# Low halves of the output weights and next-block sums formed on GpSimd instead of VectorE in the first output-layer stretch

## The chip, the cores and the metric

The kernel runs on one core of a Trainium2 chip. The metric is the device time of one execution in microseconds (us). The engines are named as the profile names them: PE is TensorE (PEld its weight loads), DVE is VectorE, ACT is ScalarE, POOL is GpSimd, SP is SyncE, which here only issues DMAs.

## The reference

The kernel computes attention through 32 packed queries per head, and two token-wise layers on the result:

```python
p_packed = sm_attn(p, k, v)
out = sm_attn(q, p_packed, p_packed)             # batch 8, heads 8, seq 576, head_dim 64
x = out.transpose(0, 2, 1, 3).reshape(4608, 512)
h = np.maximum(np.maximum(x @ w1, x @ w2), x @ w3)
x2 = h @ w_out                                   # 768 -> 512
h = x2 @ w_in                                    # 512 -> 2048
g = np.maximum(h, 0.0) + np.log1p(np.exp(-np.abs(h)))
return g @ w_out2                                # 2048 -> 512
```

Only the last two products, `x2 @ w_in` with its softplus and `g @ w_out2`, bear on the change.

## The kernel before, in words

The first 500 us or so do attention and the max-out layer, batch by batch, and store x2 in DRAM (`x2d`). After that the tokens are taken in five blocks: three of 2 x 512 columns and two of 2 x 384. In each block `layer3` (PE line 1044) forms the hidden layer, and `layer4` (PE line 1137) the output. Both use a seven-product scheme for 2x2 block matrices (`PRODUCTS`), so operands are sums of blocks: `form` (line 1101) makes the sums S1 to S4 of the hidden tiles, `sum_x2` (line 884) those of the next block's operand.

Every operand of a product is given in two parts, a high part rounded to PE's 32-bit format and a low part, the remainder. Three matmuls stand for one: high by high, high by low, low by high. The two parts are made by `split`: ACT copies the source into the high tile (line 126), and an engine, DVE unless another is named, subtracts it from the source (line 128). That second instruction is a TENSOR_TENSOR with two SBUF inputs.

`layer4` has 28 steps, v = 0 to 27, four for each product, each of 12 matmuls of 128x128 by 128x512. The operand of step v + 3 is split behind step v (`split_g`: `ghi` by ACT, `glo` by DVE); three buffers hold it, so its ACT copy waits until PE is done with step v. Eight weight tiles `wc` of the output layer (numbers 8 to 15) are used in order, one for 3.5 steps.

In the first block only, the output weights don't yet exist in split form. They are loaded from `wof` (`load_weights`, SP line 998) into `wu`, split into `wc` in a first part of 1024 columns and a second of 768 (`split_weights`), and stored for the later blocks (`put_weights`, SP line 1019). Tiles 8 and 9 are split in the layer before; the stretch splits 10 to 15, at steps 1, 4, 8, 11, 15 and 18. In the same stretch the operand of the second block is made in four parts of 128 columns: `load_x2` (SP line 923), `sum_x2` (four instructions of 128x256), `split_x2` (two ACT copies, two DVE subtractions into `x2lo`). `wu` and the operand tile `xu` share a pool of two buffers, so each next load waits until the split of the tile before in that buffer is done.

The order on every engine, the DMA queue of SP included, is the order in which this code is written (`tc.manual_schedule`). It comes from `jobs` (what is emitted behind each step) and `done` (sums and results of finished products). Behind each step come, in this order, `split_g(v + 3)`, the entries of `done`, and those of `jobs`:

```python
for v in range(NV):
    layer4(c, v)
    if v + 3 < NV:
        split_g(c, v + 3)
    for fn, *args in done.get(v, []) + jobs[v]:
        fn(*args)
```

Of the kernel before, what the change touches and what calls it, by code (L numbers as in the profile page):

```python
# [19 lines left out]
def packed_attention_maxout_softplus(  # L20
# [22 lines left out]
    nc = tc.nc  # L43
# [31 lines left out]
    FP = F2 // 2  # L75
# [45 lines left out]
    def split(src, hi, lo, engine=nc.vector):  # L121
        for _ in split_steps(src, hi, lo, engine):
            pass

    def split_steps(src, hi, lo, engine=nc.vector):
        nc.scalar.activation(out=hi, in_=src, func=AF.Copy)  # L126
        yield
        engine.tensor_tensor(out=lo, in0=src, in1=hi.bitcast(F32), op=ALU.subtract)  # L128
# [712 lines left out]
    for n in range(1, B):  # L841
        for slot in range(F1 + KC):
# [22 lines left out]
            if n + 1 == B:  # L865

                if slot == 0:
# [37 lines left out]
                    def pair_tile(s):  # L905
                        t = ring[s % 3].tile([P, 2, 7, 2, P], F32R, tag="ring", name="wc")
                        pairs[s] = t
                        return t
# [97 lines left out]
        elif s < STEP:  # L1006
            load_units(s - FP)

    def split_weights(s, part):
        if part == 0:  # L1010
            pair_tile(s)
        a, b = ((0, 4), (4, 7))[part]
        u, t = wus[s], pairs[s]
        split(u[:, a + 1 : b + 1], t[:, 0, a:b], t[:, 1, a:b])
        if part == 1:
            wus.pop(s)

# [6 lines left out]
    def get_weights(s):  # L1024
        if STEP <= s < STEP * NCH:
            r = s % STEP
            nc.sync.dma_start(
                out=pair_tile(s).rearrange("p h a k x -> p (h a k x)").bitcast(F32),
                in_=(wic[r] if r < FP else woc[r - FP]),
            )  # L1030
# [16 lines left out]
    def layer3(c, j, aside):  # L1047


        def between(at):  # L1050
            for fn, *args in aside.get(at, ()):
                fn(*args)

        w, wide = pairs.pop(STEP * c + j), BLOCKS[c][1]
        h = cp.tile([P, 10, CH], F32, tag="h", name="h")[:, :, :wide]

        def plus(o, a, ps):
            add(out=h[:, o], in0=h[:, a], in1=ps, op=ALU.add)  # L1058

        nc.scalar.activation(out=h[:, 3], in_=product(c, w, 0, 0), func=AF.Copy)  # L1060
        between(0)
        plus(0, 3, product(c, w, 1, 1))
        plus(4, 3, product(c, w, 4, 4))
        between(1)
        ps = product(c, w, 3, 3)
        plus(5, 4, ps)
        plus(6, 4, product(c, w, 5, 5))
        plus(3, 6, ps)
        between(2)
        plus(2, 6, product(c, w, 2, 6))  # L1070
        plus(1, 5, product(c, w, 6, 2))
        between(3)
        for half in range(2):
            for k in range(2):
                if j == 0:
                    g[half, k] = ap.tile(
                        [P, FP, CH], F32, tag=f"a{half}{k}", name=f"a{half}{k}"
                    )
                nc.scalar.activation(  # L1079
                    out=g[half, k][:, j, :wide], in_=h[:, 2 * k + half], func=AF.Softplus  # L1080
                )
# [5 lines left out]
    def form(c, name, u, n, engine):  # L1087


        us = slice(u, u + n)  # L1090
        a11, a12, a21, a22 = (
            g[i, k][:, us, : BLOCKS[c][1]] for i in range(2) for k in range(2)
        )
        s2 = None if name == "S3" else row(c, 1 + u // 2)
        out, in0, in1, op = {
            "S3": (a21, a11, a21, ALU.subtract),
            "S2": (s2, a22, a21, ALU.subtract),
            "S1": (a11, a11, s2, ALU.add),
            "S4": (a12, a12, s2, ALU.subtract),
        }[name]  # L1100
        engine.tensor_tensor(out=out, in0=in0, in1=in1, op=op)  # L1101
# [93 lines left out]
    with tc.manual_schedule(engines={E.PE, E.DVE, E.Activation, E.Pool, E.SP}):  # L1195
        for c in range(NCH):
            more, last = parts[c + 1], c == NCH - 1
            for j in range(FP):
                aside = {0: [], 1: [], 2: [], 3: []}
                if c == 0:  # L1200
                    if j + 2 < FP:
                        aside[0].append((sum_pair, j + 2, nc.gpsimd))
                    for part in range(2):
                        aside[1 + part].append((split_weights, j + 2, part))
                    aside[3] += [(load_weights, j + 4), (put_weights, j + 2)]
                    if j and j % 2 == 0:
                        aside[1].append((form, c, "S3", j - 2, 2, nc.vector))
                elif more:
                    for part in range(2):
                        if j == 1 + part:  # L1210
                            aside[0].append((load_x2, c + 1, part))
                        if j == 3 + part:
                            aside[1].append((sum_x2, c + 1, part, nc.gpsimd))
                if j == FP - 1:
                    for v in range(2):
                        aside[2].append((split_g, c, v))
                layer3(c, j, aside)
                if c:
                    form(c, "S3", j, 1, nc.gpsimd)
                get_weights(STEP * c + j + 3)  # L1220
            mid[c] = cp.tile([P, 10 * CH], F32, tag="h", name="mid")
            split_g(c, 2)
            jobs = {v: [] for v in range(-1, NV)}
            if c == 0:
                jobs[0].append((form, c, "S3", FP - 2, 2, nc.vector))
                for t in range(6):
                    v = 7 * t // 2 + 1
                    for part in range(2):
                        jobs[v + part].append((split_weights, FP + t + 2, part))
                    if t >= 1 and FP + t + 3 < STEP:  # L1230
                        jobs[v + 1].append((load_weights, FP + t + 3))
                    if t == 0:
                        jobs[v + 1].append((load_x2, c + 1, 0))
                    jobs[v + 2].append((put_weights, FP + t + 2))
                for part, v in enumerate((7, 12, 16, 21)):
                    jobs[v - 1].append((sum_x2, c + 1, part))
                    jobs[v].append((split_x2, c + 1, part))
                    if part + 1 < more:
                        jobs[v].append((load_x2, c + 1, part + 1))
            else:  # L1240
                for part, v in zip(range(more), (12, 14, 18, 22)):
                    if part > 1:
                        jobs[v - 1].append((sum_x2, c + 1, part))
                    jobs[v].append((split_x2, c + 1, part))
                    if part + 2 < more:
                        jobs[v].append((load_x2, c + 1, part + 2))
            for i in range(NU):
                for name, v in (("S2", 0), ("S1", 4), ("S4", 8)):
                    jobs[v + i].append((form, c, name, 2 * i, 2, nc.vector))
            done = {  # L1250
                3: [(keep_sum, c, "X", 0)],
                11: [(keep_sum, c, "X", 1)],
                13: [(out_tile, c, 0), (result, c, 0, 0, "Z", 0)],
                15: [(keep_sum, c, "Y", 2)],
                19: [(out_tile, c, 1), (result, c, 1, 1, "X", 2)],
                23: [(result, c, 0, 1, "Y", 1)],
                24: [(store, c, 0, (0, 1), [nc.sync, nc.scalar] if last else [nc.sync])],
                27: [(result, c, 1, 0, "X")],
            }
            if last:  # L1260
                done[19].append((store, c, 1, (1,), [nc.sync]))
                done[27].append((store, c, 1, (0,), [nc.sync, nc.scalar]))
            else:
                done[27].append((store, c, 1, (0, 1), [nc.sync]))
# [6 lines that stand above are left out]
                for t in range(FP):  # L1271
                    if (7 * t + 6) // 2 == v:
                        pairs.pop(STEP * c + FP + t)
                        get_weights(STEP * c + FP + t + 3)
# [36 lines left out]
```

## Time and profile before

| | us |
|---|---|
| median of 3 timed runs (lowest, highest) | 1230.43 (1228.89, 1233.96) |
| span of the profiled execution, first to last instruction | 1227.1 |
| first output-layer stretch (583.4 to 676.0) | 92.6 |
| second output-layer stretch, same 336 matmuls (752.2 to 831.0) | 78.8 |

The profile is of one execution, of which the page gives the span; its lines are read as follows. Busy time of an engine is the time in which an instruction of it ran; a row of a timeline gives start, duration and instruction, and in brackets how long the engine sat idle before it and what ended that. The duration of one instruction reaches a little over the start of the next one on the same engine; from start to start is the pitch. The span is 3.3 us below the median of the timed runs.

### The profile page before, as it was taken

The numbers are of one execution on the slowest core, as the hardware profiler recorded it, in microseconds if no ns is written. First come the engines' busy times: TensorE is split into PE (matmuls) and PEld (weight loads), VectorE is DVE, ScalarE is ACT, GpSimd is POOL, SyncE is SP. The second block draws the span as 40 slices with busy tenths as digits, with TensorE's granted clock in tenths as the row PEclk, the third lists the DMA queues.
The fourth block names the chain that finished last, engine by engine and source line by source line (L and its number), as shares of the span: only waits on it lengthen the run. The fifth ranks groups of instructions, "written<-read, shape, count | busy, mean of one in ns | idle before, by whom it ended". The sixth has DMA issues, their size and how long they took to land.

```text
span 1227.1 us, 21279 instructions
## 1 busy us (share of the span) xinstructions
PE 1202.3 (98%) x8599; PEld 1057.2 (86%) x8599; DVE 833.6 (68%) x1182; ACT 527.8 (43%) x782; POOL 217.9 (18%) x224
## 2 busy tenths in 40 slices
PE   8899999999999999999979999999999999999998
PEld 6788989898989899988757888888888899999998
DVE  2975757575757658677998447884468745884585
ACT  4744443434343434545554234542344423542343
POOL 1422312123333322240000030000310012000100
PEclk9999999999999999999999999999999999999999
DMA  9988585869695931767667955459554597668764
GB/s 236 278 216 207 152 208 174 204 200 232 194 262 171 235 104 35 266 259 261 220 244 271 327 199 205 159 201 329 188 196 171 191 357 279 241 230 320 251 254 146
DMA packets 117282, 272.25 MB, mean 222 GB/s; under 512 B 14784, under 2 KB 90304, under 8 KB 106944
## 3 DMA queue, kind: packets, MB, share of 16 engines
q1 hardware_dynamic: 110944, 260.87, 66.7%
q10 hardware_dynamic: 6240, 10.03, 2.3%
q8 instruction: 67, 1.10, 0.4%
q14 instruction: 31, 0.25, 0.1%
HBM read 211.09 MB, written 59.77 MB: 221 GB/s over the span
## 4 chain that ended last, share of the span: by engine, by line
PE 84%; DVE 8%; DMA 5%; issue 1%; ACT 1%; SPq 1%; DVEq 0%; ACTq 0%
PE ps L482 29%; PE ps L1044 27%; PE ps L1137 22%; DMA qraw<-in_q_dram 3%; DVE glo L128 2%; PE ps_w L460 2%; PE ps_s L287 1%; DVE wc L128 1%; DMA wu<-wof 1%; DMA wc<-wic 1%; DVE x2lo L128 1%; PE ps_e L331 1%; PE ps_v L358 1%; DVE a L1101 1%; PE ps_k L232 0%
## 5 line engine op out<-in xcount | busy, mean ns | idle before, releaser
L1137 PE MATMUL ps<-ghi,wc 128*128 128x512 f32 (+1 forms) x1120 | 328.3, 374 | 0.5 <-ACT ghi L126 0.5
L1044 PE MATMUL ps<-x2hi,wc 128*128 128x512 f32 (+1 forms) x1120 | 322.2, 367 | 0.9 <-DMA wc<-wic 0.9
L1058 DVE TENSOR_TENSOR h<-h,ps 128x512 f32<-128x512 f32 (+1 forms) x280 | 173.2, 633 | 155.1 <-PE ps L1044 111.5
L1137 PEld LDWEIGHTS ps<-ghi,wc 128*128 128x128 f32 x1120 | 208.4, 189 | 31.2 <-ACT ghi L126 0.9
L1044 PEld LDWEIGHTS ps<-x2hi,wc 128*128 128x128 f32 x1120 | 207.1, 188 | 27.9 <-issue 1.7
L1137 PE MATMUL ps<-glo,wc 128*128 128x512 f32 (+1 forms) x560 | 211.2, 377 | 8.6 <-DVE glo L128 8.4
L1044 PE MATMUL ps<-x2lo,wc 128*128 128x512 f32 (+1 forms) x560 | 205.6, 367 | 0.0
L1079 ACT ACTIVATE a<-h 128x512 f32<-128x512 f32 (+1 forms) x160 | 89.3, 584 | 220.2 <-DVE h L1058 209.5
L126 ACT ACTIVATE ghi<-a 128x1024 fp32r<-128x1024 f32 (+1 forms) x120 | 115.4, 972 | 100.7 <-PE ps L1137 94.2
L128 DVE TENSOR_TENSOR glo<-a,ghi 128x1024 fp32r<-128x1024 f32 (+1 forms) x120 | 131.9, 1110 | 34.6 <-ACT ghi L126 34.1
L1101 POOL TENSOR_TENSOR a<-a,a 128x512 f32<-128x512 f32 (+1 forms) x32 | 36.9, 1153 | 557.8 <-ACT a L1079 557.8
L1137 PEld LDWEIGHTS ps<-glo,wc 128*128 128x128 f32 x560 | 105.7, 189 | 30.2 <-DVE glo L128 15.1
L482 PE MATMUL ps<-a2hi,pwhi 128*128 128x288 f32 x576 | 127.6, 303 | 0.1
L482 PE MATMUL ps<-a2hi,pwlo 128*128 128x288 f32 x576 | 123.3, 296 | 0.4 <-DVE pwlo L128 0.4
L482 PE MATMUL ps<-a2lo,pwhi 128*128 128x288 f32 x576 | 123.1, 295 | 0.0
L1044 PEld LDWEIGHTS ps<-x2lo,wc 128*128 128x128 f32 x560 | 105.1, 188 | 13.1
L511 DVE TENSOR_TENSOR m<-ps,m 128x576 f32<-128x576 f32 x96 | 72.3, 753 | 48.7 <-PE ps L482 46.7
L482 PEld LDWEIGHTS ps<-a2hi,pwhi 128*128 128x128 f32 x576 | 91.7, 189 | 15.0 <-ACT m L509 5.3
L128 POOL TENSOR_TENSOR hlo<-m,hhi 128x576 fp32r<-128x576 f32 x41 | 59.2, 1445 | 237.9 <-ACT hhi L126 237.9
L128 DVE TENSOR_TENSOR pwlo<-ps_w,pwhi 128x1024 fp32r<-128x1024 f32 (+1 forms) x40 | 44.5, 1113 | 77.8 <-ACT pwhi L126 77.8
L482 PEld LDWEIGHTS ps<-a2hi,pwlo 128*128 128x128 f32 x576 | 92.5, 188 | 0.6 <-DVE pwlo L128 0.6
L482 PEld LDWEIGHTS ps<-a2lo,pwhi 128*128 128x128 f32 x576 | 92.5, 188 | 0.2 <-DVE a2lo L128 0.2
(107 smaller groups left out, 1528.2 us busy)
## 6 DMA issues: line engine op xcount, KB each, us to landing
wc<-wic SPq DMA_DIRECT2D x32, 1792.0 KB
wc<-woc SPq DMA_DIRECT2D x32, 1792.0 KB
qraw<-in_q_dram SPq DMA_DIRECT2D x112, 140.0 KB
wic<-wc SPq DMA_DIRECT2D x8, 1792.0 KB
woc<-wc SPq DMA_DIRECT2D x8, 1792.0 KB
kraw<-in_k_dram SPq DMA_DIRECT2D x96, 140.0 KB
vt<-in_v_dram SPq DMA_DIRECT2D x8, 1152.0 KB
wraw<-in_moe_w_dram SPq DMA_DIRECT2D x18, 512.0 KB
```

The lines of the kernel that those rows point to most:

```text
L126: nc.scalar.activation(out=hi, in_=src, func=AF.Copy)
L128: engine.tensor_tensor(out=lo, in0=src, in1=hi.bitcast(F32), op=ALU.subtract)
L287: nc.tensor.matmul(ps[G][cols, hh, :HS], w[rows, cols], x[rows, g, hh * HS : hh * HS + HS], start=True, stop=True,)
L331: nc.tensor.transpose(ps[: 32 * TI, i // hi, (i % hi) * P : (i % hi) * P + P], e[:, i], ident,)
L460: nc.tensor.matmul(ps[cols, G, : units * P].rearrange("p (w x) -> p w x", w=units), ppT[n][rows, cols], wsb[rows, 4 * c : 4 * c + units, g ...
L482: nc.tensor.matmul(o, w, xx, start=first, stop=last)
L511: nc.vector.tensor_tensor(out=m, in0=ps[:, :, :HS], in1=ms[n, f], op=ALU.max)
L1044: nc.tensor.matmul(out, l, r, start=(i == 0), stop=(i == len(terms) - 1))
L1058: add(out=h[:, o], in0=h[:, a], in1=ps, op=ALU.add)
L1079: nc.scalar.activation(out=g[half, k][:, j, :wide], in_=h[:, 2 * k + half], func=AF.Softplus)
L1101: engine.tensor_tensor(out=out, in0=in0, in1=in1, op=op)
L1137: nc.tensor.matmul(ps[b][:, :wide], l, r, start=first and u == 0 and head, stop=u == FP - 1 and tail, skip_group_check=not first,)
```

## The change: what it does

`split_weights` gets the engine of the subtraction as an argument, and the jobs of the first block's `layer4` pass GpSimd. The jobs for the sums of the next block's operand pass GpSimd too, and stand one step earlier (v - 2 in place of v - 1). ACT's copies, the splits of `glo` and of `x2lo` and all DMAs stay in place and order.

```diff
-    def split_weights(s, part):
+    def split_weights(s, part, engine=nc.vector):
         if part == 0:
             pair_tile(s)
         a, b = ((0, 4), (4, 7))[part]
         u, t = wus[s], pairs[s]
-        split(u[:, a + 1 : b + 1], t[:, 0, a:b], t[:, 1, a:b])
+        split(u[:, a + 1 : b + 1], t[:, 0, a:b], t[:, 1, a:b], engine)
...
-                        jobs[v + part].append((split_weights, FP + t + 2, part))
+                        jobs[v + part].append((split_weights, FP + t + 2, part, nc.gpsimd))
...
                 for part, v in enumerate((7, 12, 16, 21)):
-                    jobs[v - 1].append((sum_x2, c + 1, part))
+                    jobs[v - 2].append((sum_x2, c + 1, part, nc.gpsimd))
                     jobs[v].append((split_x2, c + 1, part))
```

On DVE, twelve rows `wc<-wu,wc` and four groups `xu<-xu` of four go; nothing else changes place. Here are its rows from step 1 on, first of before; `glo` are the low halves that PE reads, `mid` and `a_...` the sums of `form`.

```order
522 L128 TENSOR_TENSOR glo<-a_6881,ghi 128x1024
523 L128 TENSOR_TENSOR wc<-wu,wc 128x1024
524 L1101 TENSOR_TENSOR mid<-a_6885,a_6883 128x1024
525 L128 TENSOR_TENSOR glo<-a_6881,ghi 128x1024
526 L128 TENSOR_TENSOR wc<-wu,wc 128x768
527 L1101 TENSOR_TENSOR mid<-a_6885,a_6883 128x1024
528 L128 TENSOR_TENSOR glo<-a_6881,ghi 128x1024
```

In the changed kernel the same place on DVE reads so, with `glo` and `form` in turn.

```order
522 L128 TENSOR_TENSOR glo<-a_6881,ghi 128x1024
523 L1101 TENSOR_TENSOR mid<-a_6885,a_6883 128x1024
524 L128 TENSOR_TENSOR glo<-a_6881,ghi 128x1024
525 L1101 TENSOR_TENSOR mid<-a_6885,a_6883 128x1024
526 L128 TENSOR_TENSOR glo<-a_6881,ghi 128x1024
```

On POOL, which had nothing in this stretch, stand the rows that left DVE, in this order; these are the first twelve groups of sixteen, from step 1 to step 15.

```order
113 L128 TENSOR_TENSOR wc<-wu,wc 128x1024
114 L128 TENSOR_TENSOR wc<-wu,wc 128x768
115 L128 TENSOR_TENSOR wc<-wu,wc 128x1024
116 L128 TENSOR_TENSOR wc<-wu,wc 128x768
117 L884 TENSOR_TENSOR xu<-xu 128x256 x4
118 L128 TENSOR_TENSOR wc<-wu,wc 128x1024
119 L128 TENSOR_TENSOR wc<-wu,wc 128x768
120 L884 TENSOR_TENSOR xu<-xu 128x256 x4
121 L128 TENSOR_TENSOR wc<-wu,wc 128x1024
122 L128 TENSOR_TENSOR wc<-wu,wc 128x768
123 L884 TENSOR_TENSOR xu<-xu 128x256 x4
124 L128 TENSOR_TENSOR wc<-wu,wc 128x1024
```

Row 123 (the third sum) now stands ahead of row 124 (the first part of weight tile 14) on one engine, as it stood on DVE. PE, ACT and SP have the same rows in the same order as before.

## Rows read from the trace of the kernel before

**Rows 1.** The page's first part: busy us, share of the span, instructions.

```profile
PE 1202.3 (98%) x8599; PEld 1057.2 (86%) x8599; DVE 833.6 (68%) x1182; ACT 527.8 (43%) x782; POOL 217.9 (18%) x224
```

**Rows 2.** Busy time by stretch: us, then PE, PEld, DVE, ACT, POOL (instructions), clock, DMA, GB/s.

```profile
583.40:676.00 92.60, 83.79 (x339) 63.85 (x339) 82.24 (x93) 48.68 (x55) 0.00 (x0) 0.98 0.70 244
752.20:831.00 78.80, 78.80 (x337) 63.24 (x337) 66.05 (x71) 38.79 (x43) 1.29 (x1) 1.00 0.54 185
...
629.00:640.00 11.00, 6.99 (x23) 5.03 (x22) 9.97 (x13) 6.96 (x8) 0.00 (x0) 0.84 0.51 192
```

**Rows 3.** Timeline of PE in the first output-layer stretch, two of its waits.

```profile
634.98 0.50 PE L1137 MATMUL ps<-glo,wc 128*128 128x512 f32 x1 [3.55 <-DVE glo L128]
...
661.76 0.50 PE L1137 MATMUL ps<-glo,wc 128*128 128x512 f32 x1 [1.43 <-DVE glo L128]
```

**Rows 4.** Timeline of DVE in the same stretch.

```profile
589.07 2.36 DVE L128 TENSOR_TENSOR glo<-a,ghi 128x1024 fp32r<-128x1024 f32 x2 [2.17 <-ACT ghi L126]
591.36 1.22 DVE L1101 TENSOR_TENSOR a<-a,a 128x1024 f32<-128x1024 f32 x1
592.49 1.22 DVE L1101 TENSOR_TENSOR mid<-a,a 128x1024 f32<-128x1024 f32 x1
...
598.17 0.95 DVE L128 TENSOR_TENSOR wc<-wu,wc 128x768 fp32r<-128x768 f32 x1
599.04 1.22 DVE L1101 TENSOR_TENSOR mid<-a,a 128x1024 f32<-128x1024 f32 x1
...
610.12 1.55 DVE L884 TENSOR_TENSOR xu<-xu 128x256 f32<-128x256 f32 x4
611.59 1.22 DVE L1101 TENSOR_TENSOR a<-a,mid 128x1024 f32<-128x1024 f32 x1
...
613.86 2.08 DVE L128 TENSOR_TENSOR x2lo<-xu,x2hi 128x1024 fp32r<-128x1024 f32 x2
615.87 1.22 DVE L1101 TENSOR_TENSOR a<-a,mid 128x1024 f32<-128x1024 f32 x1
...
629.97 1.23 DVE L128 TENSOR_TENSOR wc<-wu,wc 128x1024 fp32r<-128x1024 f32 x1 [2.93 <-ACT wc L126]
...
638.86 0.68 DVE L1181 TENSOR_TENSOR mid<-mid,ps 128x512 f32<-128x512 f32 x1
639.57 0.71 DVE L1183 STREAM_TRANSPOSE o<-mid 128x512 f32<-128x512 f32 x1
```

**Rows 5.** Timeline of SP: first and last of the four weight loads (tiles 12 to 15).

```profile
607.96 0.36 SPq L998 DMA_DIRECT2D wu<-wof  x1
...
648.48 0.36 SPq L998 DMA_DIRECT2D wu<-wof  x1
```

**Rows 6.** The chain that ended last, in order of time, at the second of these loads.

```profile
622.52 6.33 DMA wu<-wof
628.87 1.07 ACT wc L126
```

**Rows 7.** Groups of POOL over the whole span, shapes apart: count, busy us, mean ns.

```profile
L1101 POOL TENSOR_TENSOR a<-a,a 128x512 f32<-128x512 f32 x16 | 20.7, 1292 | 324.4 <-ACT a L1079 324.4
L884 POOL TENSOR_TENSOR xu<-xu 128x256 f32<-128x256 f32 x24 | 17.3, 741 | 0.5
L1101 POOL TENSOR_TENSOR a<-a,a 128x384 f32<-128x384 f32 x16 | 16.2, 1015 | 233.4 <-ACT a L1079 233.4
```

**Rows 8.** Timelines of POOL and DVE at 531 us, first one POOL row, then with the next.

```profile
531.62 1.65 POOL L884 TENSOR_TENSOR wu<-wu 128x256 f32<-128x256 f32 x1
...
531.62 3.32 POOL L884 TENSOR_TENSOR wu<-wu 128x256 f32<-128x256 f32 x2
...
532.58 1.76 DVE L1101 TENSOR_TENSOR a<-a,a 128x1024 f32<-128x1024 f32 x1
```

**Rows 9.** Timelines of POOL and DVE at 473 us.

```profile
473.38 1.62 POOL L128 TENSOR_TENSOR hlo<-m,hhi 128x576 fp32r<-128x576 f32 x1 [2.81 <-ACT hhi L126]
...
472.50 3.31 DVE L128 TENSOR_TENSOR x2lo<-xu,x2hi 128x1024 fp32r<-128x1024 f32 x2
```

## The prediction

> **What bounds the kernel now.** I read the engines' shares first. PE is busy for 98% of the span, POOL for 18% [rows 1], so time can be won only where PE waits, and POOL looks free. Next comes busy time by stretch. The first output-layer stretch takes 92.6 us and the second one, with the same 336 matmuls, 78.8 us with a busy PE throughout [rows 2]; that is 2.814 us for each of 28 steps. So at most 13.8 us can be won. PE's timeline says when they are lost. Step 15 starts with the wait that ends at 634.98 for `glo` [rows 3]; without any loss it would start at 583.7 + 15 x 2.814 = 625.9. So 9.1 us are lost by then. The other 13 steps need 36.6 us and take 676.0 - 635.0 = 41.0: 4.4 lost, of which 1.43 are one wait [rows 3]. Another 1.8 are the clock: granted 0.84 of full speed between 629 and 640, behind the 3.55 us wait [rows 2, 3] (11 x 0.16).
>
> DVE's timeline says why `glo` is late: from 590 to 635 DVE runs its list with one pause of 2.93 us [rows 4]. Its pitch there is 1.13 us for an instruction of 1024 columns, 0.87 for one of 768, 1.47 for four sums, 2.01 for a pair of `x2lo` [rows 4]. From `glo` of step 3 (589.07 + 1.13 = 590.2) to the end of `glo` of step 15 the code has 13 `glo` and 13 forms (26 x 1.13 = 29.4), weight tiles 10 to 12 (3 x 2.0 = 6.0) and the first part of 13 (1.13), two sums (2.94), one pair of `x2lo` (2.01). With the pause that is 44.4 us, to 634.6; PE resumed at 634.98. So in this part DVE's list is the bound, and every microsecond put on it or taken off it moves PE.
>
> **The change part by part.** Off DVE's list up to step 15 go 6.0 + 1.13 + 2.94, and the pause, since DVE no longer stands behind ACT's copy of a weight tile: 13.0 us.
>
> On POOL the same instructions cost more. The stretch of before has no such row, so I price by size: two-input subtractions take 1015 ns for 384 columns and 1292 for 512 [rows 7], 2.16 ns a column. That gives 1292 + 512 x 2.16 = 2400 ns for 1024 columns and 1850 for 768; 256 columns are measured, 741 ns [rows 7]. Over the stretch POOL gets 6 x 4.25 + 16 x 0.74 = 37.3 us of work for 92.6 us, so POOL alone would manage.
>
> But DVE and POOL don't run two-input instructions side by side. At 531.62 a POOL sum takes 1.65 us instead of 0.74, while DVE works on a low half; the DVE row that follows takes 1.76 instead of 1.22 while POOL runs [rows 4, 7, 8]. The ends interlock: POOL's second sum ends at 533.27, DVE's row at 534.34, POOL's third sum at 534.94 [rows 8]. One turn of each takes 1.67 us, nearly the 1.13 + 0.74 of both in a row. It isn't special to sums: at 473.38 a low half of 576 columns on POOL, of this same line 128, turns a pair of `x2lo` on DVE from 2.08 into 3.31 us [rows 4, 9]. `glo`, the forms and `x2lo` all have two SBUF inputs. So where DVE's list is full, a POOL instruction costs DVE its own length, which is twice what DVE needed for it.
>
> The Trainium skill (GPSIMD Engine Reference, section Elementwise — side-by-side cycle accounting) gives 4497 ns for a two-input add of 2048 columns on GpSimd, and keeps such work on VectorE. By it 1024 columns would take an estimated 2.25 us and 768 1.69, and the sum below would come out some 1.2 us lower; no run here shows that yet.
>
> Bounds of a POOL turn, seen by DVE: at most its full length, at least 0.20 less (a sum costs 1.67 - 1.13 = 0.54 of 0.74 [rows 8]). A weight tile costs 3.85 to 4.25 us, a sum of four 2.2 to 3.0. Up to step 15 stand four tiles (10 to 13) and two sums: 22.9 us at most. The least, with the second part of tile 13 (1.65) falling behind `glo` of step 15, is 15.4 + 4.3 - 1.65 = 18.1. Against 13.0 taken off, that is +5.1 to +9.9 us; I take the middle, **+7.5**.
>
> From step 15 on PE needs 36.6 us for 13 steps. In that time the two engines have 12 `glo` (13.6), three pairs of `x2lo` (6.0), two tiles (8.1) and two sums (5.2): 32.9, and up to 1.75 more. DVE also has six pairs of result rows with at most one SBUF input, 1.39 us a pair [rows 4], 8.3 together, during which POOL can run. So it fits if all goes well, and is 43.0 - 36.6 = 6.4 too long if nothing overlaps. What can be late is `x2lo`: its sum was 1.47 us in one go on DVE and is now four turns with `glo` between them, 4 x 1.67 = 6.7; DVE then stands at `x2lo` with `glo` of the next step behind it, and PE waits for that. On POOL tile 14 stands behind the third sum, which waits for its loads. Against the 4.4 us lost there now, between 0 (fits, in place of the old losses others of that size) and 8 more (6.4 and one more drop of the clock, 1.8); I take **+4**.
>
> Two things cost nothing by themselves. ACT, PE and SP keep their order. The chain of weight loads (load 6.33, ACT 1.07 [rows 6], POOL's two parts 4.25, and a turn of DVE before each, 2.3) takes 13.9 us a tile, against (648.48 - 607.96) / 3 = 13.5 now [rows 5]: it keeps about today's pace. The sums a step earlier don't help, because what is short is the two engines' common time.
>
> The sum is +7.5 + 4 = +11.5 us on a span of 1227.1, which lies 3.3 us under the median; on the median, 1230.4 + 11.5 = **1242**. Its own range is +5.1 to +17.9, 1235.5 to 1248.3.
>
> **The rivals.** *DVE is relieved, as if POOL ran beside it.* Then `glo` is early throughout, and what is left is the chain of loads: its pitch falls to 6.33 + 1.07 + 4.25 = 11.7 us. With the first load no earlier than now, tile 15 is loaded at 607.96 + 3 x 11.7 = 643.1 instead of 648.48 [rows 5], and the stretch ends 5.4 us earlier: 1225. It decides if POOL's turns cost DVE less than half their length. For it speaks that POOL is idle in the stretch [rows 2]; against it, rows 8 and 9 [rows 8, 9]. The Trainium skill (Advanced Engine Details and Errata, section VectorE Performance Modes) says in a note that GpSimd blocks VectorE's two-port modes, which two-input instructions don't use, and taken alone it would give this rival; its page SBUF — State Buffer, section SBUF: two separate sides, counts two SBUF inputs too, and the trace agrees with that one. Chance 0.06.
>
> *The turns are paid, but only where DVE had room.* Up to step 15 the low end holds (+5.1), and behind it POOL runs under the result rows, so that the 4.4 us lost there now come back: +0.7, 1231. It decides if `glo` in the last 13 steps is never late. For it: 32.9 of 36.6 us fits on paper. Against it: both engines are in order, and the turns come in bursts. Chance 0.11.
>
> **How the numbers follow.** The forecast has 0.83. A measurement of this kernel tells about 0.5%, 6.2 us, from no change. Below that lies the second rival and the lowest edge of the forecast (0.03): within 0.5% 0.14, slower 0.80, faster 0.06. The range runs from 1233, which leaves out both rivals, to 1250, a little above the forecast's own end.
>
> **What would show it.** Right: POOL has 28 instructions in the stretch, of 2.4 us and more for 1024 columns, often over 3 where DVE held them up; `glo` and forms on DVE, 1.22 us now, have a mean near 1.7; PE waits for `glo` already at step 4, near 597, for some 3 us, since the first tile's turns stand ahead of `glo` of step 4; the stretch grows from 92.6 to about 104 us while the second one stays at 78.8; the last weight load is issued near 660. The first step is wrong if `glo` keeps 1.22 us beside a busy POOL; the second if the time from the start of step 15 to the end stays at 41 us or falls. A POOL subtraction of 1024 columns far from 2.4 us would make all of it wrong.

## The result and the profile after

The changed kernel takes 1241.13 us (median of 4 runs, 1239.70 to 1242.61), the kernel before 1229.66 (4 runs): 11.5 us slower, ratio 1.0088, 95% interval 1.0067 to 1.0109. The forecast was 1242.

First the same view as [rows 2]: busy time by stretch, of the changed kernel. The first line is the first output-layer stretch, the second line the second one.

```profile
587.40:690.60 103.20, 86.25 (x339) 65.28 (x338) 92.46 (x64) 48.32 (x55) 56.16 (x28) 0.95 0.62 220
766.80:845.60 78.80, 78.80 (x338) 63.27 (x337) 66.09 (x70) 38.78 (x43) 1.30 (x1) 1.00 0.55 188
```

The stretch has grown from 92.6 to 103.2 us, the next one is the same to a tenth. DVE has 28 instructions fewer in it (64 for 93; the window of before also catches the end of one more row) and is busy for 10.2 us more, although 18 us of its work have left it: a row that is held up counts as busy. (The stretch starts 4.0 us later than before: in this execution PE waited 2.05 us for a load of `vt` at 78 us and then ran at a lower clock, 0.69 on average from 80 to 90 us, long before the change's first instruction.)

To place the loss, the stretch is cut where PE gets `glo` of step 15, the cut of the prediction; here of the kernel before, then of the changed one.

```profile
583.68:634.98 51.30, 44.48 (x182) 33.34 (x181) 46.13 (x49) 30.03 (x35) 0.00 (x0) 1.00 0.64 223
634.98:675.80 40.82, 38.83 (x155) 30.11 (x156) 35.83 (x44) 18.65 (x21) 0.00 (x0) 0.96 0.77 270
```

```profile
587.64:645.55 57.91, 46.60 (x182) 35.03 (x180) 55.74 (x34) 30.29 (x35) 34.67 (x16) 0.94 0.57 198
645.55:690.48 44.93, 39.28 (x155) 29.95 (x156) 36.48 (x31) 18.03 (x20) 21.49 (x12) 0.96 0.70 247
```

Up to step 15 the change costs 57.91 - 51.30 = 6.6 us, behind it 44.93 - 40.82 = 4.1. The next view is the timeline of POOL and then of DVE at the first weight tile, where the price of a turn can be read.

```profile
596.37 2.42 POOL L128 TENSOR_TENSOR wc<-wu,wc 128x1024 fp32r<-128x1024 f32 x1 [37.73 <-ACT wc L126]
599.05 2.50 POOL L128 TENSOR_TENSOR wc<-wu,wc 128x768 fp32r<-128x768 f32 x1 [0.26 <-ACT wc L126]
```

```profile
595.31 1.22 DVE L1101 TENSOR_TENSOR a<-a,a 128x1024 f32<-128x1024 f32 x1
596.44 3.43 DVE L1101 TENSOR_TENSOR mid<-a,a 128x1024 f32<-128x1024 f32 x1
599.80 2.83 DVE L128 TENSOR_TENSOR glo<-a,ghi 128x1024 fp32r<-128x1024 f32 x1
...
614.38 1.75 DVE L128 TENSOR_TENSOR glo<-mid,ghi 128x1024 fp32r<-128x1024 f32 x1
616.05 1.76 DVE L1101 TENSOR_TENSOR a<-a,mid 128x1024 f32<-128x1024 f32 x1
```

The form of 596.44 takes 3.43 us instead of 1.22: it has stood behind POOL's 2.42. The `glo` of step 4, behind it, takes 2.83. Beside the sums (613.3 to 620.1) each row takes 1.75. A turn thus costs DVE 2.21 us for 1024 columns, 1.61 for 768 and 0.53 for a sum, the lower bounds of the prediction. PE's timeline shows what becomes of it.

```profile
602.68 0.49 PE L1137 MATMUL ps<-glo,wc 128*128 128x512 f32 x1 [2.50 <-DVE glo L128]
...
630.44 0.79 PE L1137 MATMUL ps<-glo,wc 128*128 128x512 f32 x1 [5.02 <-DVE glo L128]
...
663.35 0.51 PE L1137 MATMUL ps<-glo,wc 128*128 128x512 f32 x1 [2.19 <-DVE glo L128]
...
669.61 0.50 PE L1137 MATMUL ps<-ghi,wc 128*128 128x512 f32 x1 [0.61 <-ACT ghi L126]
...
672.18 0.49 PE L1137 MATMUL ps<-glo,wc 128*128 128x512 f32 x1 [2.08 <-DVE glo L128]
```

The first wait is that of step 4, which the kernel before didn't have. The one of 5.02 us comes after the first `x2lo`, whose DVE rows stood behind the sums and then behind weight tile 12; from 628.9, within this wait, to 635.7 the granted clock is 0.50 (1.2 GHz). The last two, at step 22, have another history, which the chain that ended last shows.

```profile
654.66 1.71 POOL xu L884
656.37 5.86 POOL wc L128 x2
662.83 4.73 DMA xu<-x2d
667.78 0.74 issue
668.52 1.05 ACT ghi L126
669.59 2.55 DVE glo L128
672.18 18.46 PE ps L1137 x71
```

The third sum on POOL ends, weight tile 14 follows in 5.86 us, and only then can tile 15 be loaded. SP issues that load at 662.24; ACT waits 8.34 us for what it brings, with `ghi` of step 22 behind. (The chain names `xu<-x2d`, issued right behind it; the ACT copy that waits reads `wu`.)

Unlike the section on the change has it, the third sum did not stand ahead of tile 14 on DVE, but between its two parts, as the timeline of DVE before shows.

```profile
643.76 1.22 DVE L128 TENSOR_TENSOR wc<-wu,wc 128x1024 fp32r<-128x1024 f32 x1
644.89 1.55 DVE L884 TENSOR_TENSOR xu<-xu 128x256 f32<-128x256 f32 x4
...
647.50 0.95 DVE L128 TENSOR_TENSOR wc<-wu,wc 128x768 fp32r<-128x768 f32 x1
```

The second sum stood in the same way between the parts of tile 13. The step earlier puts both sums ahead of the whole tile on POOL.

### The profile page after: what moved, and what is told of

Read it like the earlier page. It is cut to its first block, busy times and chain, and to the rows that moved or that the text cites. A ratio compares the mean times of both kernels' runs of the same rounds, so it can differ in the third digit from the quotient of the medians.

```text
span 1240.5 us, 21294 instructions
## 1 busy us (share of the span) xinstructions
PE 1206.8 (97%) x8599; PEld 1060.1 (85%) x8599; DVE 842.6 (68%) x1154; ACT 527.1 (42%) x782; POOL 273.9 (22%) x252
## 4 chain that ended last, share of the span: by engine, by line
PE 84%; DVE 7%; DMA 5%; issue 1%; ACT 1%; POOL 1%; SPq 1%; DVEq 0%; ACTq 0%
PE ps L482 29%; PE ps L1044 27%; PE ps L1137 23%; DVE glo L128 2%; PE ps_w L460 2%; DMA qraw<-in_q_dram 2%; PE ps_s L287 1%; DVE a L1101 1%; DMA vt<-in_v_dram 1%; DVE x2lo L128 1%; PE ps_v L358 1%; PE ps_e L331 1%; DMA wc<-wic 1%; DVE mid L1101 1%; POOL wc L128 0%
## 5 line engine op out<-in xcount | busy, mean ns | idle before, releaser
L128 DVE TENSOR_TENSOR glo<-a,ghi 128x1024 fp32r<-128x1024 f32 (+1 forms) x120 | 143.4, 1207 | 39.5 <-ACT ghi L126 39.0
L482 PEld LDWEIGHTS ps<-a2hi,pwhi 128*128 128x128 f32 x576 | 91.7, 189 | 15.1 <-ACT m L509 5.3
```

What stands on the lines that cost most here:

```text
L482: nc.tensor.matmul(o, w, xx, start=first, stop=last)
```

## The experiments

All ratios are to the kernel before, timed beside it on the same chip.

**Each half alone.** Low halves of the weights on GpSimd, sums on VectorE as before:

```diff
-                    jobs[v - 2].append((sum_x2, c + 1, part, nc.gpsimd))
+                    jobs[v - 1].append((sum_x2, c + 1, part))
```

> Only the low halves of the weights are on GpSimd; the sums stay on VectorE, where they stood. Theory (a GpSimd turn holds up VectorE's two-input instructions for its own length): a weight tile costs VectorE 2.22 + 1.65 = 3.87 us instead of 2.0; up to step 15 that is +3.7 to +5.3 us, behind it 0 to +3; together about 6 us slower than before, half of the change's loss. Rival (the loss is the chain of weight loads, lengthened by GpSimd's slower subtractions): the chain is the same as in the full change, so all of its loss is here, about 11 us slower than before.

Measured: 1234.94 us against 1231.30, ratio 1.0032 (1.0012 to 1.0052), 3.6 us slower. (Its profiled execution took 1243.23 us, the longest of its 12 runs, so no stretch is read from it; a row of it stands in the last section.) The other half, the sums on GpSimd and the low halves on VectorE:

```diff
-                        jobs[v + part].append((split_weights, FP + t + 2, part, nc.gpsimd))
+                        jobs[v + part].append((split_weights, FP + t + 2, part))
```

> Only the sums of the next block's operand are on GpSimd, two steps ahead of their split; the low halves stay on VectorE. Theory: four turns of a sum cost VectorE 4 x 0.54 = 2.2 us instead of 1.47, and the split waits for four turns between which other rows stand; +1.4 us up to step 15 and 0 to +4 behind it: 2 to 5 us slower than before. Rival (chain of weight loads): that chain is as before, VectorE is relieved by 5.9 us: no loss, 0 to 3 us faster.

Measured: 1233.58 us, ratio 1.0019 (0.9996 to 1.0041), 2.3 us slower. The low halves alone don't carry all of the loss, as the rival wants; the sums come out at the theory's lower end, though their interval just reaches no change. Their loss isn't all of the theory's making: in the profile POOL's first sum takes 10.75 us (last section), ACT stands at `x2hi` behind the sums, and PE waits 2.22 and 1.69 us behind that. Both together cost more (1.0088) than the two added (1.0051); the difference, 4.5 us, is about as large as the uncertainty of the three intervals together. What the full change has and neither half has is sums and tiles one behind the other on POOL.

**Where the sums stand.** The full change, with the sums one step later:

```diff
-                    jobs[v - 2].append((sum_x2, c + 1, part, nc.gpsimd))
+                    jobs[v - 1].append((sum_x2, c + 1, part, nc.gpsimd))
```

> The full change, but the sums on GpSimd stand one step ahead of their split, as before, instead of two. Theory (the two engines' common time is short): where the sums stand matters little, 8 to 14 us slower than before, as the change. Rival (the earlier place of the sums puts them ahead of a weight tile on GpSimd and this is what costs): most of what the full change loses beyond its two halves goes, 4 to 7 us slower than before.

Measured: 1240.06 us against 1229.75, ratio 1.0096 (1.0077 to 1.0115), 10.3 us slower, as the change. So the earlier step alone isn't the cause, as the theory has it. That the sums stand in line with the tiles isn't excluded as a cause: in this order the second and third sum stand between the two parts of a tile, as they did on DVE, and the second parts of tiles 13 and 14 still wait for a sum. The last load comes 15.8 us after the one before (17.8 in the change), but ACT now stands at `x2hi` for the sums, as here for the second one, with `ghi` behind; PE's waits of 1.37 and 1.68 us for `ghi` follow.

```profile
638.02 1.06 ACT L126 ACTIVATE x2hi<-xu 128x1024 fp32r<-128x1024 f32 x1 [2.88 <-POOL xu L884]
```

**VectorE relieved without GpSimd.** The twelve low halves are written by ACT, as copies of the weights:

```diff
-        split(u[:, a + 1 : b + 1], t[:, 0, a:b], t[:, 1, a:b])
+        if aside:
+            for half in range(2):
+                nc.scalar.activation(out=t[:, half, a:b], in_=u[:, a + 1 : b + 1], func=AF.Copy)
```

> The kernel before, where the low halves of the six weight tiles are written by a second ScalarE copy instead of VectorE's subtraction (they come out as copies of the weights): VectorE is relieved without any GpSimd turn. Theory: VectorE's list up to step 15 falls by 6.0 + 1.1 and the pause of 2.9 us, of which PE can get back the 9.1 us that it loses there; 8 to 12 us faster than before, ratio 0.990 to 0.9935. Were something else than VectorE's list the bound (the loads, or ScalarE, which gets some 10 us more): 0 to 4 us faster.

Measured: 1221.34 us, ratio 0.9912 (0.9885 to 0.9939), 10.0 us faster. The whole stretch in its profile, then its part up to step 15 with some 2 us more:

```profile
583.88:665.63 81.75, 79.61 (x337) 62.97 (x336) 70.38 (x80) 58.12 (x67) 0.00 (x0) 1.00 0.80 280
583.88:629.00 45.12, 44.57 (x190) 35.41 (x189) 40.31 (x43) 35.39 (x42) 0.00 (x0) 1.00 0.72 256
```

PE is busy for 44.57 of the first 45.12 us: what it lost there is gone. So VectorE's list was the bound of that part, and the change had the right target; GpSimd's turns took more than the relief was worth.

**GpSimd's turns without the relief.** The kernel before, with twelve GpSimd instructions on top, on which no load waits:

```diff
         split(u[:, a + 1 : b + 1], t[:, 0, a:b], t[:, 1, a:b])
+        if again:
+            low = t[:, 1, a:b]
+            nc.gpsimd.tensor_tensor(
+                out=low, in0=low.bitcast(F32), in1=low.bitcast(F32), op=ALU.add
+            )
```

> The kernel before, with GpSimd adding each weight low half to itself behind VectorE's subtraction (it comes out doubled): twelve GpSimd instructions of the change's sizes, on which no load waits. Theory: VectorE's list stays and is held up by each turn, 13 to 15.5 us up to step 15 and 4 to 8 behind it: 17 to 23 us slower than before, more than the full change. Rival (chain of weight loads): the chain is untouched, so no difference, at most 2 us.

Measured: 1244.51 us against 1231.30, ratio 1.0101 (1.0072 to 1.0129), 13.2 us slower. That excludes the rival, but it is under the expected 17, and it isn't all of the theory's making. PE's timeline has a wait of another kind:

```profile
610.88 1.22 PE L1142 MATMUL ps<-ghi,wc 128*128 128x512 f32 x2 [7.44 <-POOL wc L1017]
```

PE waited for the tile that POOL rewrites, because POOL's first instruction took 16.2 us. So the run was made again with a subtraction of two different tiles:

```diff
-                out=low, in0=low.bitcast(F32), in1=low.bitcast(F32), op=ALU.add
+                out=low, in0=t[:, 0, a:b].bitcast(F32), in1=low.bitcast(F32), op=ALU.subtract
```

> As the run with twelve GpSimd instructions beside VectorE's, but each takes the low half off the high half (subtraction of two different tiles, as in the change; the low halves come out wrong). In the run with the additions, which lost 13 us, the first GpSimd instruction took 16.2 us and PE waited 7.4 us for it, so only part of its loss was VectorE being held up. If that one was particular to the addition or to one tile read twice, all turns are now 2 to 3.5 us, PE waits for the operand's low halves alone, and the loss is 8 to 15 us. If GpSimd can be kept out for long by VectorE's unbroken list, a row of 8 us or more stands in the first part again.

Measured: 1245.84 us against 1230.75, ratio 1.0132 (1.0115 to 1.0149), 15.1 us slower. The long first instruction is there again; below, the timeline of POOL, of DVE beside it, and of PE.

```profile
596.15 16.63 POOL L1017 TENSOR_TENSOR wc<-wc 128x1024 fp32r<-128x1024 f32 x1 [41.42 <-PE ps L1142]
```

```profile
597.07 1.22 DVE L128 TENSOR_TENSOR glo<-a,ghi 128x1024 fp32r<-128x1024 f32 x1
598.21 0.95 DVE L128 TENSOR_TENSOR wc<-wu,wc 128x768 fp32r<-128x768 f32 x1
...
609.03 1.22 DVE L128 TENSOR_TENSOR glo<-mid,ghi 128x1024 fp32r<-128x1024 f32 x1
610.17 2.89 DVE L884 TENSOR_TENSOR xu<-xu 128x256 f32<-128x256 f32 x2
```

```profile
612.83 1.22 PE L1142 MATMUL ps<-ghi,wc 128*128 128x512 f32 x2 [7.90 <-POOL wc L1017]
...
632.80 0.50 PE L1142 MATMUL ps<-glo,wc 128*128 128x512 f32 x1 [3.93 <-DVE glo L128]
...
647.30 0.80 PE L1142 MATMUL ps<-glo,wc 128*128 128x512 f32 x1 [3.85 <-DVE glo L128]
```

From 597.07 to 610.2 every DVE row keeps its usual length, and POOL gets its turn only when DVE's second sum stands back. So in these two runs more than a third of PE's waiting in the stretch is for POOL's tile (7.90 of some 23 us in the second run); most of the rest is the expected one for `glo`. They show that two-input instructions of the two engines exclude each other, in either direction; as a measure of the turns alone they aren't clean.

**One input on GpSimd.** As the run with the low halves alone, but POOL copies the weights instead of subtracting:

```diff
+            nc.gpsimd.tensor_copy(out=t[:, 1, a:b], in_=u[:, a + 1 : b + 1])
```

> The low halves of the weights as GpSimd copies of the weights (one SBUF input; they come out wrong), the sums on VectorE. Beside the run with the same twelve places as two-input subtractions on GpSimd, which came out 4 us slower than before. Theory A (any GpSimd instruction that reads SBUF holds up VectorE's two-input rows for its length): a copy of 1024 columns is some 1.2 to 1.6 us by the one-input rows of 512 columns (0.65 to 0.83), so a tile costs VectorE 2.0 to 2.8 us, about what was taken off; 3 us faster to 2 us slower than before. Theory B (only two-input GpSimd rows hold it up): VectorE is as free as with ScalarE's copies, 8 to 10 us faster than before, and VectorE's rows keep 1.22 us beside the copies.

Measured: 1221.69 us against 1230.61, ratio 0.9935 (0.9911 to 0.9959), 8.9 us faster by the medians. The time is what theory B gives, but the rows are those of theory A; POOL first, then DVE:

```profile
583.26 1.56 POOL L1016 CAST wc<-wu 128x1024 fp32r<-128x1024 f32 x1 [29.04 <-PE ps L1048]
...
594.86 1.08 POOL L1016 CAST wc<-wu 128x1024 fp32r<-128x1024 f32 x1 [8.27 <-DMA woc<-wc]
```

```profile
593.81 1.22 DVE L128 TENSOR_TENSOR glo<-a,ghi 128x1024 fp32r<-128x1024 f32 x1
594.95 2.06 DVE L1105 TENSOR_TENSOR mid<-a,a 128x1024 f32<-128x1024 f32 x1
```

The sum at 594.95, which begins beside the copy at 594.86, takes 2.06 us instead of 1.22, so a one-input row of POOL holds DVE up too. But it is 1.08 us long and not the 1.2 to 1.6 expected. By DVE's rows the second, third and fourth of the six tiles cost DVE 1.3 to 1.5 us each where 2.0 to 2.8 were expected, the first 0.8, and the last two nothing: one falls beside result rows, which keep their 0.68 and 0.71 us, the other in a pause of DVE. The copies also wait for no ACT copy, only for their load; what that alone is worth wasn't measured. So the expectation had the right mechanism in theory A and sized it wrongly.

**Work moved inside VectorE's list.** All on VectorE, as before, with part of the list at later steps:

```diff
-                for t in range(6):
-                    v = 7 * t // 2 + 1
+                for t, v in enumerate((1, 4, 8, 11, 16, 20)):
...
-                for part, v in enumerate((7, 12, 16, 21)):
+                for part, v in enumerate((10, 15, 21, 24)):
...
+                late = {"S2": (0, 1, 2, 3), "S1": (5, 6, 7, 8), "S4": (10, 13, 17, 18)}
                 for name, v in (("S2", 0), ("S1", 4), ("S4", 8)):
-                    jobs[v + i].append((form, c, name, 2 * i, 2, nc.vector))
+                    at = late[name][i] if c == 0 else v + i
+                    jobs[at].append((form, c, name, 2 * i, 2, nc.vector))
```

> The kernel before, all on VectorE, with work moved from the first twelve steps to later ones: the last two weight tiles at steps 16 and 20, the operand's parts at 10, 15, 21, 24, the forms S1 one step later and S4 at 10, 13, 17, 18. Theory (VectorE's list is the bound up to step 15 and has room behind it): three forms and one sum leave the first part, 4.9 us, and the pause of 2.9 may go; 4 to 7 us faster than before. Rival (VectorE is short over the whole stretch, its list of 82 us against 78.8 of PE, so that moving work inside it wins nothing): within 2 us of before.

Measured: 1224.54 us against 1229.75, ratio 0.9959 (0.9944 to 0.9973), 5.2 us faster, with no work taken off VectorE. Its two parts of the stretch, cut as above:

```profile
586.47:631.83 45.36, 43.36 (x182) 33.59 (x181) 41.37 (x42) 27.52 (x32) 0.00 (x0) 1.00 0.69 246
631.83:672.82 40.99, 37.79 (x156) 28.83 (x157) 40.57 (x51) 21.30 (x24) 0.00 (x0) 1.00 0.80 282
```

The first part falls from 51.30 to 45.36 us, the second stays (40.99 for 40.82) with DVE now busy in nearly all of it. The same order with the change's GpSimd work in it (both edits together):

> The moved order of the run before it, with the change's low halves and sums on GpSimd. Theory: the common list is some 14 us longer than VectorE's alone (33 us of turns for 18 us taken off), and no order hides that: 6 to 11 us slower than the moved order on VectorE, about 0 to 6 us slower than before. Rival (the change loses only through the order of its turns in the first twelve steps): within 3 us of the moved order on VectorE.

Measured: 1235.93 us, ratio 1.0059 (1.0044 to 1.0074): 11.4 us slower than the moved order on VectorE, as much as the change costs in the old order. So the order didn't make the loss. The moved order with only the last two tiles' low halves on GpSimd:

```diff
+                        low = nc.gpsimd if t > 3 else nc.vector
-                        jobs[v + part].append((split_weights, FP + t + 2, part))
+                        jobs[v + part].append((split_weights, FP + t + 2, part, low))
```

> The moved order on VectorE, with only the low halves of the last two weight tiles on GpSimd, where VectorE has its result rows, which take one SBUF input. Theory: four turns, 7.7 us, for 4.0 us taken off, part of them under 9 us of result rows: 0 to 3 us slower than the moved order on VectorE. Rival (GpSimd is of use where VectorE isn't full): 1 to 3 us faster than it.

Measured: 1227.20 us, ratio 0.9988 (0.9973 to 1.0002), 2.7 us slower than the moved order, with intervals that just touch. Even there no use of GpSimd shows. The last run moves a little more on VectorE:

```diff
-                for part, v in enumerate((10, 15, 21, 24)):
+                for part, v in enumerate((10, 16, 21, 25)):
...
-                late = {"S2": (0, 1, 2, 3), "S1": (5, 6, 7, 8), "S4": (10, 13, 17, 18)}
+                late = {"S2": (0, 1, 2, 3), "S1": (5, 6, 7, 9), "S4": (10, 12, 17, 18)}
```

> The moved order on VectorE, with the operand's parts at steps 10, 16, 21, 25, and the forms S1 at 5, 6, 7, 9 and S4 at 10, 12, 17, 18. Theory (VectorE's list bounds up to step 15, and is nearly full behind it): one sum and a pair of low halves go one step later and one form one step earlier; 0 to 2 us faster than the moved order, 5 to 7 us faster than before. Rival (the last part's low halves come too late for the next block's first product): 0 to 3 us slower than the moved order.

Measured: 1222.92 us against 1230.61, ratio 0.9940 (0.9922 to 0.9958), 7.7 us faster than the kernel before by the medians. The two moved orders were timed on different chips and their intervals overlap, so which is better stays open; both beat both kernels.

## Why the prediction was right

*VectorE's list bounds PE up to step 15.* Shown by the run that relieves it without GpSimd (PE's losses there go, 10.0 us faster) and by the moved order (5.2 us faster with the same work).

*POOL and DVE exclude each other in two-input instructions.* Shown by the rows at 596 us and, with VectorE's work kept, by the long POOL rows in the runs with GpSimd instructions on top. In the first output-layer stretch of the changed kernel `glo<-a,ghi` has a mean of 1696 ns where 1.7 us were expected:

```profile
L128 DVE TENSOR_TENSOR glo<-a,ghi 128x1024 fp32r<-128x1024 f32 x24 | 40.2, 1696 | 7.3 <-ACT ghi L126 7.3
```

*+7.5 us up to step 15, +4 behind it.* 6.6 and 4.1 in the profiled executions. The first is under the middle because the turns cost their lower bounds: four tiles at 2.21 + 1.61 and two sums at 4 x 0.53 are 19.5 us, less the 13.0 taken off 6.5. A low half of 1024 columns takes 2.42 us where nothing is in its way; 2.40 had been put from rows of 384 and 512 columns. The 2.25 estimated from the Trainium skill (GPSIMD Engine Reference, section Elementwise — side-by-side cycle accounting) is 7% under that row.

*The first rival, relief as if POOL ran beside DVE,* is excluded by the rows; relief itself was worth more than it was given, 10.0 us and not 5.4, for the low halves alone. The note of the Trainium skill that spoke for it (Advanced Engine Details and Errata, section VectorE Performance Modes) doesn't cover these instructions. The page SBUF — State Buffer of the Trainium skill, section SBUF: two separate sides, does, and the trace agrees with it at 3.43 for 1.22 us.

*The second rival, nothing late behind step 15,* is excluded by the 44.93 us there. Its premise holds in part: result rows keep their 0.68 us beside POOL's tile 15 (at 672.05).

*What was mis-sized.* The step "the chain of weight loads keeps about today's pace", 13.9 us a tile. The four issues of the changed kernel are at 613.40 and 662.24 at their ends, 16.3 us a tile. The last takes 17.8, because the third sum stands ahead of tile 14 on POOL and is stretched by DVE; why the two before it took 15.1 and 15.9 wasn't traced. That chain is what PE waits for at step 22 (0.61 + 2.08 us). Behind step 15 PE waits 5.57 us where it waited 1.99 before; 2.69 of these 5.57 are step 22, and only the 2.19 at 663.35, behind an `x2lo` pair of 4.84 us, and 0.69 are the lateness of `x2lo` and `glo` on which the +4 rested. So +4 is right in size, but in good part by a term that had been put at nothing. The drop of the clock, priced at 1.8 us, came elsewhere: the 0.50 from 628.9 to 635.7 lies up to step 15, where DVE's rows follow each other without a pause and set the time, so nothing shows that it cost anything there; behind step 15 the mean clock is 0.96 in both kernels.

*Luck.* The stretch grew by 10.6 us, and the ratio of 1.0088 is 10.8 us; low turns were made up for by the chain of loads. That the medians differ by just the 11.5 of the forecast is chance: the interval of the ratio is 8 to 13 us.

*Left open.* Why the two halves add up to less than the whole; the sums and tiles in line on POOL are an argument, not a measurement. How often POOL is kept out for long (last section) in the executions without a profile isn't known either, and so neither is its part in these times.

## What to carry to other kernels

Before work is given to an idle engine, look in the trace for a place where that engine and the full one run the same kind of instruction at once, and read whether the rows keep their length. If they exclude each other, count both engines' instructions as one list: here 18 us off VectorE's list put some 31 us back on it, by the measured turns (6 x 3.82 and 16 x 0.53). When an engine is the bound in one part of a stretch and has room in the next, moving work inside its own list is cheaper than moving it off.

## What was not expected of the hardware

Neither engine's turn is assured. As a rule POOL got in at DVE's next instruction, but in four of the profiled executions one POOL row was kept out for 10 to 14 us, while nine or more DVE rows ran one behind the other at their usual pitch: in the two kernels with extra GpSimd instructions (16.18 us, and the row of 16.63 us above), and in each half of the change. Below, POOL's timeline with the low halves alone, then with the sums alone, where the usual lengths are 2.42 and 0.74 us.

```profile
622.13 13.10 POOL L128 TENSOR_TENSOR wc<-wu,wc 128x1024 fp32r<-128x1024 f32 x1 [8.81 <-ACT wc L126]
```

```profile
601.95 10.75 POOL L884 TENSOR_TENSOR xu<-xu 128x256 f32<-128x256 f32 x1 [47.62 <-DMA xu<-x2d]
```

Behind the first of these the next weight load is issued late, at 637.24, and PE waits 7.82 us for `ghi`; that is the execution of 1243.23 us. The profile of the full change has no such row, and what distinguishes these places was not found. And a POOL copy with one input, 1.08 us for 1024 columns against 2.42 for the subtraction, holds DVE's two-input rows up as well (a sum of 1024 columns took 2.06 us instead of 1.22).
